# Gated recurrence and top-1 experts on one core: held blank writes, eleven x rows, an early tile of expert 0, and the general path's loop behind the experts

## The chip, the cores and the metric

The kernel runs on one core of a Trainium2 chip. The metric is the device time of one execution in microseconds, from the first to the last instruction of the program with what starts and ends it. Before the change three runs took 733.5, 734.44 and 731.06 us (median 733.5). A further run was profiled: it took 731.12 us, and its span in the profile, first to last instruction, is 729.4 us. All positions in time below are microseconds of that span.

## The reference

Two blocks follow each other.

```
# gateloop: B, H, S, D = 4, 8, 768, 48
mag = sqrt(a_re^2 + a_im^2); a *= min(mag, 0.999) / (mag + 1e-6)
for t in range(S):                       # a complex state D x D per (b, h)
    S_re, S_im = a_re*S_re - a_im*S_im + k[t] v[t]^T, a_re*S_im + a_im*S_re
    y[t] = q[t] . S_re
# x = y as (B*S, H*D) = (3072, 384)
# switch, top 1 of E = 8 experts, F = 1024
logits = x @ w_gate; e = argmax(logits); gate = softmax(logits)[e]
out = gate * (relu(x @ w1[e]) @ w2[e])
```

All data are fp32. Each of the 3,072 tokens goes through exactly one expert.

## The kernel before

**Attention stage.** The recurrence is computed in chunks of 128 steps (C = 6 chunks per sequence). For one batch b at a time, `front` (L369) scans the gates on VectorE: fifteen steps of multiplies, 576 and 288 wide, and one add each; `fix` (L413) carries the result over blocks, once for each of the three tiles t of 128 rows of heads x dimension, `fold` (L432) multiplies q and k with the scanned gates and writes the products `pk`, from which DMAs on SyncE load the tiles `KX` and `QX`, and `attention` (L491) does the scores, masks and outputs on TensorE for each group of heads. `load_gates` (L336) brings the gates a_re and a_im of a batch in four pairs of DMAs, and `limit` (L343) normalises them on ScalarE and VectorE.

Each chunk's outputs are gathered into an `xf` row buffer: 128 tokens by 384 values plus the gate and the token number. There are `ROWS = C + 2 = 8` of these buffers (L36), taken in turn: chunk number b*C + c uses buffer (b*C + c) % ROWS, so that a buffer is written again eight chunks later, and then only when its move has read it.

**Router.** `send` (L616) takes the logits of a batch, finds expert, gate and a place (slot) for each token in the DRAM table `sorted_x`, and moves each chunk's 128 rows there by an indirect DMA on POOL (`away`, L661 to L671). Batches 0 to 2 are sent whole, batch 3 in three pieces of three, two and one chunks (L201). `free_row` holds how many rows of each expert are taken so far. Each expert has room for CAP = 448 rows. Rows that no token fills must be blank, and so, once before the first move, eight DMAs on POOL write blank rows over the eight experts' places (L681, 675.5 KB each, from the tile `empty`). In the list of steps each blank write is put after a step of batch 1's front, but that order is only a due time for the planner: in the program the writes wait only for the memset of `empty`.

**Order.** None of this is issued as it is written: every step is an `Op` with an engine, a modelled duration, what it needs and which buffers it reuses. `in_time` (L85) simulates the engines, and the steps are emitted in the order of the simulated starts (L704). `InOrder` (L127) keeps that order on each engine. Its one line, L135, is therefore the line of nearly all planned instructions in the profile; tiles tell them apart. Within an engine's queue an instruction that waits holds back all behind it.

**Junction.** Behind the last send, `fine` says whether the fast path's assumptions held, and one matmul (`bank<-ones_f,fine`) sums it to `trips`, 0 or 1. The weights of experts 0 to 2 are fetched ahead (L700). Then `load` (L712) brings expert 0's 448 rows: three tiles of 128 on SyncE, the half tile in two DMAs on ScalarE's queue. `values_load` (L746) reads `trips` into a register of each engine. `with tc.For_i(0, n_gen, 1)` (L1007) repeats the whole computation in a general way when `trips` is 1; with the inputs here it runs no time.

**Expert stage** (L1015 to L1054). For each expert: `turned` (L723) transposes the 448 rows on TensorE (twelve transposes), 24 products with w1 give h in eight tiles of 448 columns (`h_ps`), which ScalarE (even) and VectorE (odd) evict with relu to `ht`; three o tiles of 384 columns and one half tile (`o_ps`) follow, each scaled by the gate on eviction and moved to `out` by an indirect DMA on POOL (`to_out`, L736; the token numbers are in `to`). The next expert's rows are loaded and turned inside the loop, and `fetch(e + 3)` brings weights. An fp32 matmul is two records in the trace. PSUM comes from pools: 2 buffers for transposes, 4 for h, 2 for o.

Of the kernel before, what the change touches and what calls it, by code (L numbers as in the profile page):

```python
# [19 lines left out]
C = S // 128  # L20
# [15 lines left out]
ROWS = C + 2  # L36
CAP = 448
LEAST = 1e-20
# [100 lines left out]
def gateloop_then_moe(ctx, tc, q, k, a_re, a_im, v, wg, w1, w2, out):  # L139
# [106 lines left out]

    with ExitStack() as att:
        one = att.enter_context(tc.tile_pool(name="one", bufs=1))
        bank = att.enter_context(tc.tile_pool(name="bank", bufs=1, space=PSUM))
# [18 lines left out]
        QXs = [buf(f"QX{i}", C, 256) for i in range(RING)]  # L268
        KTs = [buf(f"kt{i}", 3, 128) for i in range(2)]
        for i in range(RING):  # L270
            nc.gpsimd.memset(KXs[i][R2:128, :], 0.0)
            nc.gpsimd.memset(QXs[i][R2:128, :, :], 0.0)
            nc.gpsimd.memset(QXs[i][0:R2, :, 128 + R2:], 0.0)
# [22 lines left out]
        ps = [bank.tile([128, 512], FP32, name=f"bank{i}") for i in range(8)]  # L296
# [194 lines left out]
        def attention(b, g):  # L491
# [24 lines left out]
            for c in range(C):  # L516
# [51 lines left out]
                if c < C - 1:  # L568
                    ws, st_readers = ring("st", 2)

                    def turned(c=c, wk=wk, st=st):
                        for i in range(n):
                            vals = vb[c].rearrange("p h e -> p (h e)")[:, first[i]:first[i] + 128]
                            if c > 0:
                                T.matmul(sp_ps[:, i, :], lhsT=QX[i][:, c, 128:], rhs=sts[st[0]][:, i, :], start=True, stop=False)
                            T.matmul(sp_ps[:, i, :], lhsT=KTs[wk][:, i, :], rhs=vals, start=(c == 0), stop=True)
# [35 lines left out]
        def send_all():  # L612
            while sent_later:
                send(*sent_later.pop(0))

        def send(k, b, c0, n, lg):  # L616
# [40 lines left out]
            state["free row"], state["count"] = f, [f]  # L657
            state["lg"] = [d]
            moves = []
            for i in range(n):  # L660
# [8 lines left out]
                move = pool_dma(8.0, away, [s, m, *state["blank"]] + state["row", b, c0 + i])  # L669
                moves += [move, m]  # L670
                state["xf", (b * C + c0 + i) % ROWS] = [move, state["x row", b, c0 + i]]  # L671
            state["sent", k % 2], state["sent"] = [s, gate, f, *moves], [s, gate, f]
# [3 lines left out]
        for b in range(B):  # L676
            steps = front(b, range(G))
            fixed = [fix(t) for t in range(G)]
            if b == 1:

                state["blank"] = [pool_dma(8.0, lambda e=e: nc.gpsimd.dma_start(  # L681
                    sorted_x[e * N:e * N + CAP].rearrange("(u p) w -> p u w", p=64), bc(empty[:, None, :], [64, CAP // 64, WS])), [o])
                    for e, o in enumerate((steps + sum(fixed, []))[3::2][:E])]
                send_all()
# [14 lines left out]
        dve(1, lambda: V.tensor_scalar(out=trips, in0=ps[7][0:1, 511:512], scalar1=127.5, scalar2=None, op0=ALU.is_lt), [o])  # L699
        for e in range(3):  # L700
# [7 lines left out]
    with ExitStack() as ms:  # L708
# [4 lines left out]
        def load(e, xs, half_queue=nc.sync):  # L713
            r = e * N
            nc.sync.dma_start(xs[:, 0:TT, :], sorted_x[r:r + TT * 128].rearrange("(t p) w -> p t w", p=128))
# [4 lines left out]
        def room():  # L720
            return xp.tile([128, TT + 1, WS], FP32, name="xs")

        def turned(xs):  # L723
            xt = mp.tile([128, DT, CAP], FP32, name="xt")
            for d in range(DT):
                ps = psX.tile([128, CAP], FP32, name="xt_ps")
                for i in range(TT + 1):
                    n = min(128, CAP - i * 128)
                    T.transpose(ps[:, i * 128:i * 128 + n], xs[0:n, i, d * 128:d * 128 + 128], ident[0:n, 0:n])
                if d == 1:  # L730
                    nc.scalar.copy(xt[:, d, :], ps)
                else:
                    nc.vector.tensor_copy(xt[:, d, :], ps)
            return xt
# [10 lines left out]
        xs = load(0, room(), nc.scalar)  # L745
        n_gen = nc.values_load(trips[0:1, 0:1], min_val=0, max_val=1, skip_runtime_bounds_check_because="0 or 1")  # L746


        def general():
            gs = ExitStack()  # L750
            gen = gs.enter_context(tc.tile_pool(name="gen", bufs=1))
            with ExitStack() as fs:
                fp = fs.enter_context(tc.tile_pool(name="fp", bufs=1))
                fps = fs.enter_context(tc.tile_pool(name="fps", bufs=1, space=PSUM))
                lg_all = gen.tile([128, NT, E], FP32, name="lg_all")
                zrow = fp.tile([1, W], FP32, name="zrow")
                nc.vector.memset(zrow, 0.0)
                nc.sync.dma_start(x_hbm[N:N + 1, :], zrow)
                BG = B * G
                state = fp.tile([128, 2, BG, D], FP32, name="state")  # L760
                nc.gpsimd.memset(state, 0.0)

                own_i = fp.tile([128, G, H], I32, name="own_i")
                nc.gpsimd.iota(own_i, pattern=[[128, G], [-D, H]], base=0, channel_multiplier=1)
                own_f = fp.tile([128, G, H], FP32, name="own_f")
                nc.vector.tensor_copy(own_f, own_i)
                own = fp.tile([128, G, H], FP32, name="own")
                nc.vector.tensor_scalar(out=own, in0=own_f, scalar1=0.0, scalar2=None, op0=ALU.is_ge)
                nc.vector.tensor_scalar(out=own_f, in0=own_f, scalar1=float(D), scalar2=None, op0=ALU.is_lt)
                tt(own, own, own_f, ALU.mult)  # L770
                x_tok = x_hbm[0:N, 0:DM].rearrange("(b s) (h e) -> s h b e", b=B, e=D)
                with tc.For_i(0, S // BL, 1) as i0:
                    a = fp.tile([128, 2, BG, BL], FP32, name="fa")
                    qk = fp.tile([128, 2, BG, BL], FP32, name="fqk")
                    for b in range(B):
                        for t in range(G):
                            for o, src in ((a[:, 0], a_re), (a[:, 1], a_im)):
                                nc.sync.dma_start(o[:, b * G + t, :], src[b].rearrange("p j (t m) -> t m p j", t=G)[t, ds(i0, 1)])
                            for u, src in enumerate((q, k)):
                                nc.sync.dma_start(qk[:, u, b * G + t, :], src[b, :, t].rearrange("p j m -> m p j")[ds(i0, 1)])  # L780
                    vt = fp.tile([128, BG, BL, D], FP32, name="vt")
                    for b in range(B):
                        for t in range(G):
                            for h, p0, n, d0 in segments(t):
                                src = v[b].rearrange("(m j) (h w) -> m h j w", j=BL, w=D)[ds(i0, 1), h]
                                nc.sync.dma_start(vt[p0:p0 + n, b * G + t], src.to_broadcast([n, BL, D]))
                    af = a.rearrange("p u n t -> p u (n t)")
                    sq = fp.tile([128, 2, BG * BL], FP32, name="fsq")
                    mag = fp.tile([128, BG * BL], FP32, name="fmag")
                    den = fp.tile([128, BG * BL], FP32, name="fden")  # L790
                    nc.scalar.activation(sq, af, func=ACT.Square)
                    tt(mag, sq[:, 0, :], sq[:, 1, :], ALU.add)
                    nc.scalar.activation(mag, mag, func=ACT.Sqrt)
                    nc.vector.tensor_scalar_add(den, mag, 1e-6)
                    nc.vector.reciprocal(den, den)
                    stt(den, mag, 0.999, den, ALU.min, ALU.mult)
                    tt(af, af, bc(den[:, None, :], list(af.shape)), ALU.mult)
                    for t in range(BL):
                        shape = [128, BG, D]

                        def col(x, u):
                            return bc(x[:, u, :, t:t + 1], shape)
                        z = {}
                        for x in range(2):
                            for y in range(2):
                                z[x, y] = fp.tile(shape, FP32, name=f"fz{x}{y}")
                                tt(z[x, y], state[:, x], col(a, y), ALU.mult)
                        vv = fp.tile(shape, FP32, name="fvv")
                        tt(vv, vt[:, :, t, :], col(qk, 1), ALU.mult)
                        tt(state[:, 0], z[0, 0], z[1, 1], ALU.subtract)  # L810
                        tt(state[:, 1], z[0, 1], z[1, 0], ALU.add)
                        tt(state[:, 0], state[:, 0], vv, ALU.add)
                        tt(vv, state[:, 0], col(qk, 0), ALU.mult)
                        yt = fps.tile([H, B, D], FP32, name="yt")
                        for g in range(G):
# [281 lines left out]
```

## Time and profile before

| engine | busy us | share of the span | instructions |
|---|---|---|---|
| TensorE (PE) | 570.0 | 78% | 3050 |
| TensorE weight load (PEld) | 423.8 | 58% | 3050 |
| VectorE (DVE) | 366.3 | 50% | 726 |
| ScalarE (ACT) | 297.9 | 41% | 926 |
| GpSimd (POOL) | 92.5 | 13% | 101 |

DMA moved 89.79 MB at a mean of 123 GB/s. The mean granted clock of TensorE was 0.955. The stages, by the trace: the first matmul starts at 100.90, the last one of the attention stage at 398.18, the expert stage's first transposes at 408.47, the last out DMA is issued at 721.81. From one expert's last out DMA to the next one's, in steady state, are 38.75 us.

How to read it: the page cuts the span into 40 slices and gives busy tenths of each engine. A group row gives a line, an engine, an operation and its tiles (out<-in), then busy us and mean ns. A timeline row gives start, duration, engine, line, operation and tiles, and in brackets the idle time of that engine ahead of it and what released it ("<-DMA x" is a transfer, "<-ACT x" an instruction of ScalarE). A row of a window gives the stretch, its length, then the busy time (and number) of PE, PEld, DVE, ACT and POOL, TensorE's granted clock, the busy share of the 16 DMA engines and GB/s. SPq and POOLq are the queues from which SyncE and POOL issue DMAs.

### The profile page before, as it was taken

How to read it: one execution, taken by the hardware profiler on the slowest of the kernel's cores; microseconds unless marked ns; L12 is line 12 of the kernel's file. 1: busy time of each engine (PE TensorE's matmuls, PEld its weight loads, DVE VectorE, ACT ScalarE, POOL GpSimd, SP SyncE). 2: the span in 40 equal slices, each digit the busy share in tenths (PEclk: the TensorE clock that was granted, in tenths of full speed). 3: DMA queues.
4: the chain of work that ended last, by engine and by line, in shares of the span. 5: the costliest groups of instructions: out<-in, count | busy, mean ns of one | idle time of the engine just before them, and what ended most of it. 6: DMA issues, size and time to landing. Idle time of an engine off the chain costs nothing. (4 is left out here: it accounts for less than half of the span.)

```text
span 729.4 us, 8993 instructions
## 1 busy us (share of the span) xinstructions
PE 570.0 (78%) x3050; PEld 423.8 (58%) x3050; DVE 366.3 (50%) x726; ACT 297.9 (41%) x926; POOL 92.5 (13%) x101
## 2 busy tenths in 40 slices
PE   0000049985479989988996599999999999999995
PEld 0000039985469978987896355565655555555553
DVE  3929999999979999997413110201011111111010
ACT  4525369976869689568653110101010101001000
POOL 9300000000340023003003002010101111010101
PEclk9999999995879999998999699999999999999999
DMA  6982078327661578369921322323232324020000
GB/s 192 222 193 65 21 198 208 107 67 187 161 190 51 131 197 268 113 148 225 310 123 67 91 86 76 131 82 129 102 141 109 141 100 148 12 68 12 18 12 24
DMA packets 59718, 89.79 MB, mean 123 GB/s; under 512 B 5885, under 2 KB 48015, under 8 KB 57616
## 3 DMA queue, kind: packets, MB, share of 16 engines
q1 hardware_dynamic: 54640, 73.94, 34.6%
q0 software_dynamic: 4864, 15.00, 7.1%
q8 instruction: 26, 0.43, 0.2%
q10 hardware_dynamic: 160, 0.20, 0.1%
q14 instruction: 28, 0.23, 0.1%
HBM read 55.10 MB, written 15.78 MB: 97 GB/s over the span
## 5 line engine op out<-in xcount | busy, mean ns | idle before, releaser
L135 PE MATMUL bank<-QX,KX 128*128 128x224 f32 (+1 forms) x384 | 89.2, 369 | 113.1 <-DMA KX<-pk 100.9
L135 PE MATMUL h_ps<-xt,big 128*128 128x448 f32 x384 | 148.1, 546 | 0.0
L135 PE MATMUL o_ps<-big,ht 128*128 128x384 f32 (+1 forms) x640 | 147.9, 424 | 0.0
L135 PEld LDWEIGHTS bank<-QX,KX 128*128 128x128 f32 x384 | 70.4, 208 | 116.8 <-issue 100.9
L135 PEld LDWEIGHTS o_ps<-big,ht 128*128 128x128 f32 (+1 forms) x640 | 90.1, 169 | 56.1 <-issue 4.7
L135 PEld LDWEIGHTS h_ps<-xt,big 128*128 128x128 f32 x384 | 73.0, 192 | 71.3 <-issue 71.2
L135 PE MATMUL bank<-st,QX 128*128 128x128 f32 x576 | 110.2, 279 | 2.2 <-ACT st L135 2.2
L135 ACT ACTIVATE big<-big 128x576 f32<-128x576 f32 (+2 forms) x92 | 79.2, 871 | 43.0 <-DVE big L135 23.2
L135 PEld LDWEIGHTS bank<-st,QX 128*128 128x128 f32 x576 | 88.4, 195 | 3.1 <-ACT st L135 3.1
L135 PE MATMUL bank<-vb,am 128*128 128x128 f32 x384 | 74.0, 284 | 14.0 <-ACT xf L135 13.9
L135 ACT ACTIVATE QX<-diag,KX 96x48 f32<-96x48 f32 x320 | 80.4, 328 | 7.3 <-DMA KX<-pk 7.1
L662 POOL DMA_INDIRECT sorted_x<-xf,slot x24 | 38.8, 1616 | 336.8 <-DVE big L135 170.0
L1030 ACT ACTIVATE ht<-h_ps 128x448 f32<-128x448 f32 x32 | 17.4, 544 | 131.9 <-PE h_ps L135 131.9
L1028 DVE TENSOR_SCALAR ht<-h_ps 128x448 f32<-128x448 f32 x32 | 20.0, 624 | 99.2 <-PE h_ps L135 99.0
L135 PEld LDWEIGHTS bank<-vb,am 128*128 128x128 f32 x384 | 59.7, 196 | 16.6 <-ACT xf L135 16.1
L135 DVE TENSOR_TENSOR big<-big,big 128x576 f32<-128x576 f32 (+1 forms) x72 | 62.9, 884 | 0.5
L135 DVE TENSOR_TENSOR big<-big 128x288 f32<-128x288 f32 (+2 forms) x104 | 60.9, 600 | 1.1 <-ACT big L135 0.6
L135 PE MATMUL bank<-vb,kt 128*128 128x128 f32 x320 | 59.3, 277 | 1.7 <-ACT kt L135 1.7
L1041 ACT ACTIVATE yo<-o_ps,xs 128x384 f32<-128x384 f32 x16 | 9.3, 581 | 124.8 <-PE o_ps L135 124.8
L135 DVE TENSOR_TENSOR am<-bank,causal 128x256 f32<-128x256 f32 (+1 forms) x120 | 42.7, 362 | 34.0 <-PE bank L135 33.9
L737 POOL DMA_INDIRECT out_dram<-yo,to x24 | 23.4, 974 | 279.3 <-ACT yo L1041 245.8
L135 PEld LDWEIGHTS bank<-vb,kt 128*128 128x128 f32 x320 | 47.6, 192 | 2.3 <-ACT kt L135 1.9
(105 smaller groups left out, 500.5 us busy)
## 6 DMA issues: line engine op xcount, KB each, us to landing
big<-in_moe_w_dram SPq DMA_DIRECT2D x16, 1536.0 KB, 6.6
KX<-pk SPq DMA_DIRECT2D x48, 146.2 KB, 4.4
QX<-pk SPq DMA_DIRECT2D x48, 144.0 KB, 3.8
sorted_x<-empty POOLq DMA_DIRECT2D x8, 675.5 KB, 11.7
xs<-sorted_x SPq DMA_DIRECT2D x8, 579.0 KB, 8.4
big<-in_a_re_dram SPq DMA_DIRECT2D x16, 288.0 KB, 3.4
big<-in_a_im_dram SPq DMA_DIRECT2D x16, 288.0 KB
qt<-in_q_dram SPq DMA_DIRECT2D x12, 384.0 KB, 4.7
```

The lines of the kernel that those rows point to most:

```text
L135: return lambda *a, **kw: self.tc.keep_in_program_order(f(*a, **kw))
L662: move = nc.gpsimd.indirect_dma_start(out=sorted_x[:, :], out_offset=bass.IndirectOffsetOnAxis(ap=slot[:, i:i + 1], axis=0), in_=xfs[(b * ...
L737: move = nc.gpsimd.indirect_dma_start(out=rows, out_offset=bass.IndirectOffsetOnAxis(ap=index, axis=0), in_=y, in_offset=None, bounds_chec ...
L1028: nc.vector.tensor_scalar_max(ht[:, f, :], h, 0.0)
L1030: nc.scalar.activation(ht[:, f, :], h, func=ACT.Relu)
L1041: nc.scalar.activation(y, o, func=ACT.Copy, scale=xs[:, i, DM:DM + 1])
```

## The change

There are four edits.

1. *Blank writes.* Each of the eight DMAs gets a semaphore dependency on the VectorE instruction that was emitted last before it. The steps that they are put behind change too: the adds 2, 5, 8, 11 and 14 of batch 1's front and the last step of each of its three fixes.
2. *Buffers.* Eleven xf rows in place of eight; a row of `QX` becomes 224 wide in place of 256, and the memset of its pad (six on POOL) goes. The matmul that read the pad as weights reads 32 columns of the next chunk in its place, into outputs that are not used. The modelled time of a move goes from 8 to 10.
3. *Early tile.* After batch 2's send, `free_row` of expert 0 is raised to at least 128 (one more VectorE instruction), so that batch 3 writes no row below 128. `load_early` reads these 128 rows on SyncE, the last item of the attention stage in that queue, into the free tail of a weight buffer; `turn_early` turns them (three transposes, one ScalarE copy), ahead of the last send's ranks on TensorE. Behind the `fine` matmul follow the tile's h (24 products of 128 columns), four evictions each on ScalarE and VectorE, its o (eight of 384), the scaling on VectorE and an out DMA. Expert 0 then has 320 rows left: nine transposes, h of 320 columns, two tiles and the half one.
4. *Loop.* The loop of the general path and the function stand behind the experts, and `values_load` stands in the pass of expert 6. PSUM pools become eight banks that both stages share, with the same counts. The rewrite of blank rows inside the general path goes.

On VectorE's queue the order behind `trips` is now: `to_e`, early evictions f1 and f3, the `to` of expert 0, f5 and f7, the `to` of expert 1, then y_e and the copies of `xt`. On SyncE the loads of experts 0 and 1 follow each other directly.

```diff
-ROWS = C + 2
+ROWS = C + 5
+EARLY = 128
...
-        QXs = [buf(f"QX{i}", C, 256) for i in range(RING)]
+        QXs = [buf(f"QX{i}", C, 128 + R2) for i in range(RING)]
...
-            nc.gpsimd.memset(QXs[i][0:R2, :, 128 + R2:], 0.0)
...
+        def load_early():
+            l = dma(5.0, lambda: Q.dma_start(xs_e, sorted_x[0:EARLY]), state["moves"], state["z", 0] + state["z", 1])
+            state["early"] = l
+        def turn_early():
+            def across_early():
+                for d in range(DT):
+                    T.transpose(px_ps[:, d, :], xs_e[:, d * 128:d * 128 + 128], ident)
+            px = pe(6, across_early, [state["early"]], state.get("px", []), first=B * G)
+            c = act(DM, lambda: A.copy(xt_e, px_ps), [px], first=6)
...
+            if b == B - 2:
+                f = dve(1, lambda: V.tensor_scalar_max(free_row[:, k + 1, 0:1], free_row[:, k + 1, 0:1], float(EARLY)), [f])
...
-                move = pool_dma(8.0, away, [s, m, *state["blank"]] + state["row", b, c0 + i])
+                move = pool_dma(10.0, away, [s, m, *state["blank"]] + state["row", b, c0 + i])
...
-                    for e, o in enumerate((steps + sum(fixed, []))[3::2][:E])]
+                def blank(e):
+                    step = next(i for i in reversed(nc.cur_bb.bb.instructions) if i.engine == nc.vector.engine)
+                    tc.add_manual_dep(nc.gpsimd.dma_start(sorted_x[e * N:e * N + CAP].rearrange("(u p) w -> p u w", p=64),
+                                                          bc(empty[:, None, :], [64, CAP // 64, WS])).ins, step.name,
+                                      mybir.DependencyInfo(mybir.DependencyClass.Sync, mybir.DependencyReason.DATA), reason="not before")
+                state["blank"] = [pool_dma(8.0, lambda e=e: blank(e), [o]) for e, o in enumerate((steps[1::3] + sum(fixed, [])[1::2])[:E])]
...
+        def first_tile(e):
+            return EARLY // 128 if e == 0 else 0
+        def bank_of(kind):
+            own = {"x": (6, 7), "h": (2, 3, 4, 5), "o": (0, 1)}[kind]
...
+        to_e = mp.tile([128, 1], I32, name="to_e", bufs=1)
+        nc.vector.tensor_copy(to_e, xs_e[:, DM + 1:WS])
+        for i in range(2):
+            h = bank_of("h").rearrange("p (f w) -> p f w", w=128)
+            for f in range(4):
+                for d in range(DT):
+                    T.matmul(h[:, f, :], lhsT=w1t[:, d, (4 * i + f) * 128:(4 * i + f) * 128 + 128], rhs=xt_e[:, d, :],
+                             start=(d == 0), stop=(d == DT - 1))
+            for f in range(4):
+                if f % 2:
+                    nc.vector.tensor_scalar_max(ht_e[4 * i + f], h[:, f, :], 0.0)
+                else:
+                    nc.scalar.activation(ht_e[4 * i + f], h[:, f, :], func=ACT.Relu)
+        o = bank_of("o")[:, 0:DM]
+        for f in range(FT):
+            T.matmul(o, lhsT=ht_e[f], rhs=w2t[:, f, :], start=(f == 0), stop=(f == FT - 1))
+        nc.vector.tensor_scalar_mul(y_e, o, xs_e[:, DM:DM + 1])
+        to_out(y_e, out, to_e)
...
-        with tc.For_i(0, n_gen, 1):
-            general()
-            load(0, xs)
...
+            if e == E - 2:
+                n_gen = nc.values_load(trips[0:1, 0:1], min_val=0, max_val=1, skip_runtime_bounds_check_because="0 or 1")
...
+    with tc.For_i(0, n_gen, 1):
+        general()
```

## The prediction

> **What bounds the kernel now.** First the busy tenths in 40 slices (18.2 us each):
>
> ```profile
> PE   0000049985479989988996599999999999999995
> DVE  3929999999979999997413110201011111111010
> PEclk9999999995879999998999699999999999999999
> DMA  6982078327661578369921322323232324020000
> ```
>
> Three stages with different limits. Up to slice 17 VectorE is full but for one hole in slice 2, while TensorE starts late (100.9 us) and has holes; slices 18 to 20 are TensorE's; from slice 22 the experts keep TensorE full. So a gain counts if it shortens VectorE's chain before about 330 us, or TensorE's time after it. I then read the timelines at the holes.
>
> The hole of slice 2 (VectorE's and ScalarE's timelines, SyncE's issues, the issue table, one window with the DMA share next to last):
>
> ```profile
> 28.73 0.38 SPq L135 DMA_DIRECT2D big<-in_a_re_dram  x1
> 29.15 2.35 SPq L135 DMA_DIRECT2D big<-in_a_im_dram  x1
> 50.44 1.74 ACT L135 ACTIVATE big<-big 128x1152 f32<-128x1152 f32 x2 [14.89 <-DMA big<-in_a_im_dram]
> 51.63 0.76 DVE L135 SCALAR_TENSOR_TENSOR big<-big 128x576 f32<-128x576 f32 x1 [12.82 <-ACT big L135]
> sorted_x<-empty POOLq DMA_DIRECT2D x8, 675.5 KB, 11.7
> 26.00:28.00 2.00, 0.00 (x0) 0.00 (x0) 2.00 (x5) 0.73 (x3) 0.00 (x0) 1.00 1.00 198
> ```
>
> Gate loads issued at 29 us land at 50; behind them VectorE waits 12.82 us. Meanwhile the eight blank writes, issued from 18.25 us, fill the DMA engines (share 1.00).
>
> The xf rows and the junction to the experts (VectorE, POOL, TensorE):
>
> ```profile
> 206.57 0.76 DVE L135 SCALAR_TENSOR_TENSOR big<-big 128x576 f32<-128x576 f32 x1 [3.51 <-ACT big L135]
> 193.80 8.50 POOL L662 DMA_INDIRECT sorted_x<-xf,slot  x1 [169.72 <-DVE big L135]
> 398.18 0.19 PE L135 MATMUL bank<-ones_f,fine 128*1 128x1 f32 x2 [0.93 <-DVE fine L135]
> 408.47 3.45 PE L135 MATMUL xt_ps<-ident,xs 128*128 128x128 f32 x12 [10.11 <-SPq L1007]
> 411.86 19.92 PE L135 MATMUL h_ps<-xt,big 128*128 128x448 f32 x48
> 398.00:399.00 1.00, 0.19 (x2) 0.09 (x2) 0.27 (x2) 0.00 (x0) 0.69 (x2) 0.54 0.23 87
> 414.00:415.00 1.00, 1.00 (x2) 0.34 (x1) 0.00 (x0) 0.00 (x0) 0.00 (x0) 0.50 1.12 401
> 416.00:417.00 1.00, 1.00 (x4) 0.44 (x4) 0.00 (x0) 0.55 (x1) 0.00 (x0) 1.00 0.05 6
> ```
>
> TensorE stands still for 10.11 us: last moves, xs load, loop. The windows (column before the DMA share: TensorE's clock) show half clock until 415.
>
> **What the Trainium skill says.** "TensorE: Matmul & The Clock Gate", What's actually happening: TensorE runs at half clock after an idle window and returns to full after some 3.4 us of continuous work. The trace agrees: 0.54 at 398, 0.50 at 414, 1.00 by 416, about 3.2 us after the first h matmul. "DMA: Bandwidth & Descriptors", Issuing engines are not separate DMA queues: transfers of all issuers share the same engines. It agrees: SyncE's gate loads took 21 us beside POOL's blanks. "Runtime: NRT & Kernel Launch", Instruction fetch mechanics: a jump outside the fetched instructions waits for a fetch. The trace can't separate that from the loop's other costs.
>
> **Part 1, blanks held** (semaphores on VectorE's adds 2, 5, 8, 11, 14 of batch 1's front and on the three fixes). Queue 0 holds 43.8% of the 16 engines in 0 to 60 us: 26.3 us of full DMA, 3.3 per blank. Bytes issued on hardware queues before 28.7 us are about 4.3 MB; at the 314 to 367 GB/s of these stretches they drain by some 22 us. The load of 28.7 then lands after some 3.4 us, as a_re does in the issue table, and the next (issued 38.84) by 43, before ScalarE needs it at 44.5. The whole hole goes: **−12.8**, and the chain behind it is solid until 203 us.
>
> The same 26.3 us come back at 117 to 173 (old clock). There the DMA share has mean 0.49 over 116 to 176, so they fit as a whole; in 116 to 140 alone five blanks (16.5 us) meet 10.3 us of free time, so KX, QX and gate loads run late by up to 6 us. TensorE has such slack (it waits for VectorE 6 us at 169 to 175), VectorE has less. From 0 to +6; I take **+1.5**, since the stretch 144 to 160 is nearly empty (shares 0.07 to 0.23) and lets the queue drain. Queued behind the waiting blanks on POOL are only batch 0's moves, due at 193.8 − 12.8 = 181; the last blank is released near 173 − 12.8 = 160 and landed in 11.7 us: 172. Hidden. The six pad memsets that go (0.26 us each) lay on POOL, which has no work then: nothing.
>
> **Part 2, eleven xf rows, narrower QX.** ScalarE waits 4.18 us for row 0's move (at 205.6), and VectorE 3.51 us behind it. With eleven rows reuse comes at batch 1's chunk 5, not 2; but on ScalarE's queue the copy that waits stands at nearly the same place (row 289, was 286), with one activation of the gates now ahead of it. Below, a gain of all 3.51 us (a little more if TensorE's hole of 12.55 counts); above 0. I take **−2**.
>
> **Part 3, early tile.** Added on TensorE behind the `fine` matmul: 24 h products of 128 columns (48 records at 0.1115 us, the full-clock pitch of that width) = 5.35, and 8 o products of 384 (16 at 0.321) = 5.15: 10.5 us. Removed from expert 0: three transposes, an h pass of 128 of 448 columns (18.0 → 12.9 us) and one o tile (5.15). The early work lies in the hole that was idle: its data are in before the last moves. At half clock for its first 3 to 3.4 us it needs some 3 us more: from 398.4 to 411.9. Then nine transposes (1.7), h 12.9, turning expert 1 (1.3), two tiles 10.3, half tile 2.6, about 0.6 of gaps: 441.3, against 452.7 now (its last out DMA): **−11.4**. Ends: −14.1 if the clock stays high; −6 if VectorE's queue holds it. On ScalarE the half loads (issued at 401.8, after the last moves) stand ahead of ht_e f0. On VectorE `to_e` waits for the same moves, the `to` of experts 0 and 1 stand ahead of ht_e f5, f7 and y_e and wait for the xs loads (402 to 407 or later). Early h takes until 405 or so, which covers most of these waits.
>
> The added early transposes (three), ScalarE copy, VectorE maximum and out DMA lie before the last send or behind TensorE: about nothing. The early load on SyncE is last in its queue behind the fetches; its 128 rows land during batch 3, which is TensorE's 64 us. The maximum can shift expert 0's slots by empty rows only.
>
> **Part 4, loop behind the experts.** VectorE's loop steps took 0.8 us (407.43 to 408.20), plus a jump; SyncE waited 3.8 us in it. At the end nothing covers it: 0.5 to 4, I take **+1.4**. The load of `trips` (684 ns on TensorE at 398.6) now stands between experts 6 and 7: 0 to 0.7, **+0.5**. Banks keep their counts (2, 4, 2): nothing. Its removal at 407 is in part 3.
>
> **Sum:** −12.8 + 1.5 − 2 − 11.4 + 1.4 + 0.5 = −22.8 against the profiled span 729.4: 706.6. That run took 731.1 (1.7 more than its span): 708.3. From the median 733.5: 710.7. Forecast **709.5**.
>
> **Rivals.**
> - *Junction only half filled* (VectorE's `to` ahead of the early evictions, SyncE's two loads side by side: about 1.2 MB): −6 instead of −11.4: 715. For: the order of VectorE's queue; against: the loads were short in the trace (DMA busy 403 to 406).
> - *More than the sum*: clock high (−14.1), all 3.5 at 203, no collision: 709.5 − 2.7 − 1.5 − 1.5 = 704; with TensorE's small holes near 251 to 279, 701.
> - *Collision*: KX, QX and gate loads late beside the blanks by more than the slack, at most all 16 us of overrun and later stalls; at +10 to +12: 719. For: share 1.05 at 120 to 124; against: 0.49 in the mean.
> - *The hold doesn't do what it says*: the blanks still start early enough to meet the gate loads, or other loads fill the DMA alone: no −12.8, no +1.5: 721.
> - *Slower than before*: the blanks become the new wait. All moves of batch 0 wait for all eight, and POOL issues in order; if the eighth lands after 181, each us more holds the first move (8.5 us itself), then ScalarE's xf copy, then VectorE and TensorE. To end above 733.5 needs 24 us of such delay, a landing near 205, which is 45 us from release; before, the slowest landed in 26 us under full load. Then about 738.
>
> **How the numbers follow.** Forecast 0.42, half-filled junction 0.18, more 0.14, collision 0.12, no hold 0.08, slower 0.04; 0.02 for the unforeseen. The range from 700 to 722 leaves out the slower case and tails, about 0.15. About 0.5% (3.7 us) is what a measurement can tell from no change. Faster 0.93, same 0.03, slower 0.04.
>
> **What would show it.** Part 1: no idle time of VectorE before 51 us, gate loads landing in about 3.4 us, blanks from some 105 us on. Wrong if a hole appears in VectorE between 105 and 170 or the first move is later than 182. Part 2: no xf copy waiting for a move. Part 3: h matmuls of 128 columns right behind `fine`, expert 0's last out DMA about 11 us closer to `fine` than the present 54; wrong if o_ps waits for VectorE or ScalarE between them. Part 4: the time from the last out DMA to the end, now 6.6 us (722.8 to 729.4), grows by 1 to 2. Wrong altogether if some expert's step of 38.75 us changes, or batch 3's 64 us grow.

## The result, and the profile after

Four runs of the changed kernel took 724.67 us in the median (721.07 to 725.23), four of the kernel before on the same chip 732.9: a ratio of 0.9878, with a 95% interval from 0.9838 to 0.9919. The change is faster by some 8 us; the forecast was 709.5, and 724.67 lies above the range that ended at 722. Its profiled execution took 725.23 us with a span of 723.3, against 729.4 before: 6.1 less in the two traces that are compared here. (The trace of before is of a run 1.8 us under its median; the sums below are those of the two traces.)

The busy tenths of the page, after the change:

```profile
PE   0000099875799659997998899999999999999991
DVE  3999999898999999995423111111010101011100
PEclk9999999986999879999999999999999999999996
DMA  5321579469841775478921324242423312010000
```

VectorE's hole in slice 2 is gone and TensorE starts most of a slice earlier. But TensorE shows new dents in slices 8, 13 and 14, and in the last slice it stands still, at a falling clock. Five marks in the traces cut the difference into pieces. "am, batch 1" is the first product with `am` of batch 1, the moment when TensorE has that batch's scores, masks and state together.

| mark | before | after | difference | change of it |
|---|---|---|---|---|
| first matmul | 100.90 | 89.38 | −11.5 | −11.5 |
| am, batch 1 | 180.62 | 176.59 | −4.0 | +7.5 |
| `fine` matmul | 398.18 | 394.13 | −4.05 | 0.0 |
| expert 0's last out DMA | 452.95 | 439.52 | −13.4 | −9.4 |
| expert 7's last out DMA | 721.81 | 708.75 | −13.1 | +0.4 |
| end | 729.40 | 723.26 | −6.1 | +6.9 |

So two pieces came about as forecast (start and junction), and two costs were far larger: 7.5 us between the first matmul and batch 1, and 6.9 at the end.

**Between the first matmul and batch 1.** The timelines of POOL, ScalarE, VectorE and TensorE of the changed kernel (start, duration, engine, line, operation; in brackets the idle time ahead and its releaser):

```profile
106.99 0.92 POOL L710 DMA_DIRECT2D sorted_x<-empty  x1 [91.94 <-DVE am L136]
112.16 0.74 POOL L710 DMA_DIRECT2D sorted_x<-empty  x1 [4.25 <-DVE am L136]
...
167.69 0.70 POOL L710 DMA_DIRECT2D sorted_x<-empty  x1 [10.93 <-DVE fl L136]
127.28 1.16 ACT L136 ACTIVATE big<-big 128x1152 f32<-128x1152 f32 x1 [3.62 <-DMA big<-in_a_im_dram]
128.47 0.76 DVE L136 SCALAR_TENSOR_TENSOR big<-big 128x576 f32<-128x576 f32 x1 [2.51 <-ACT big L136]
170.51 3.80 ACT L136 ACTIVATE QX<-diag,KX 96x48 f32<-96x48 f32 x16 [2.46 <-DMA KX<-pk]
171.21 5.55 PE L136 MATMUL bank<-QX,KX 128*128 128x224 f32 x16 [11.19 <-ACT QX L136]
```

and TensorE's row for the same scores in the kernel before:

```profile
175.43 5.35 PE L135 MATMUL bank<-QX,KX 128*128 128x224 f32 x16 [6.11 <-ACT QX L135]
```

The hold works as written: the first blank goes at 107, the last at 168. What was a wait for a gate load at 51 us is now a wait for gate loads at 127 and for KX at 170, and TensorE stands idle for 11.19 us ahead of batch 1's scores (6.11 before). Not all of this idle time is the late KX: a run below, without a blank in this stretch, still has 9.35 us of it.

**The junction**, TensorE's and VectorE's timelines, and the window of 400 to 410 (TensorE's clock stands just before the DMA share):

```profile
395.69 5.73 PE L136 MATMUL bank<-big,big 128*128 128x128 f32 x42
401.25 3.39 PE L136 MATMUL bank<-big 128*128 128x384 f32 x10
406.37 0.91 PE L136 MATMUL bank<-big 128*128 128x384 f32 x2 [1.73 <-DVE big L799]
408.41 1.92 PE L136 MATMUL bank<-ident,xs 128*128 128x128 f32 x9
405.88 0.16 DVE L155 SCALAR_TENSOR_TENSOR to<-xs,upper 128x1 int32<-128x1 f32 x1 [4.20 <-DMA xs<-sorted_x]
406.03 0.28 DVE L799 TENSOR_SCALAR big<-bank 128x128 f32<-128x128 f32 x1
400.00:410.00 10.00, 8.16 (x37) 4.99 (x35) 2.46 (x10) 1.50 (x5) 0.49 (x1) 1.00 0.50 138
```

The early tile fills the hole. Its first products run from 394.25 at half clock, but in this window the clock is full. VectorE's `to` of expert 0 stood ahead of an early eviction and waited 4.20 us for xs, and the o tile waited behind it.

**The end**, POOL's timeline and then the view of the loop's line (durations in ns: least, median, most; then the first and last start in us) and of the program's last line:

```profile
708.75 0.97 POOL L777 DMA_INDIRECT out_dram<-yh,to  x1 [1.58 <-DVE yh L845]
...
L1108 POOLq EVENT_SEMAPHORE  x17: 17/43/43, 709.2 to 716.9; - x17
L1108 POOLq COMPARE_BRANCH  x3: 38/41/49, 709.2 to 717.0; - x3
L1108 POOLq INC_SWDGE_SEM  x1: 1467/1467/1467, 711.8 to 711.8; - x1
...
L1147 POOLq DRAIN  x3: 40/103/5302, 717.1 to 723.0; - x3
```

POOL enters the loop at 709.2, waits for the last out DMA to land (711.7), steps its DMA semaphores for 1.47 us, jumps, goes through twelve semaphores and leaves at 717.0. The other engines wait in the loop too, so it acts as a barrier. Only then does its last drain begin, which takes 5.3 us. Before the change the drain began right behind the last out DMA:

```profile
L1093 POOLq DRAIN  x3: 40/247/6516, 721.6 to 729.1; - x3
```

### The profile page after: what moved, and what is told of

Same layout as the page of the kernel before. It is cut to its first block, busy times and chain, and to the rows that moved or that the text cites. A ratio compares the mean times of both kernels' runs of the same rounds, so it can differ in the third digit from the quotient of the medians.

```text
span 723.3 us, 9083 instructions
## 1 busy us (share of the span) xinstructions
PE 568.9 (79%) x3098; PEld 427.5 (59%) x3098; DVE 369.4 (51%) x733; ACT 296.2 (41%) x929; POOL 85.2 (12%) x95
## 5 line engine op out<-in xcount | busy, mean ns | idle before, releaser
L136 PE MATMUL bank<-big,ht 128*128 128x384 f32 (+1 forms) x624 | 142.7, 423 | 0.0
L136 PE MATMUL bank<-xt,big 128*128 128x448 f32 (+1 forms) x384 | 141.3, 528 | 0.0
L136 PEld LDWEIGHTS bank<-big,ht 128*128 128x128 f32 (+1 forms) x624 | 87.0, 168 | 53.9 <-issue 4.7
L136 PEld LDWEIGHTS bank<-xt,big 128*128 128x128 f32 x384 | 72.3, 190 | 65.5 <-issue 61.8
L824 DVE TENSOR_SCALAR ht<-bank 128x448 f32<-128x448 f32 (+1 forms) x32 | 19.4, 607 | 97.6 <-PE bank L136 97.4
L826 ACT ACTIVATE ht<-bank 128x448 f32<-128x448 f32 (+1 forms) x32 | 17.0, 530 | 125.9 <-PE bank L136 125.9
L136 DVE TENSOR_TENSOR big<-big,big 128x576 f32<-128x576 f32 (+1 forms) x72 | 62.9, 884 | 0.4
L136 PE MATMUL bank<-vb,kt 128*128 128x128 f32 x320 | 61.4, 286 | 0.9 <-ACT kt L136 0.9
L136 DVE TENSOR_TENSOR am<-bank,causal 128x256 f32<-128x256 f32 x120 | 42.7, 363 | 34.9 <-PE bank L136 26.7
L837 ACT ACTIVATE yo<-bank,xs 128x384 f32<-128x384 f32 x15 | 8.7, 580 | 120.6 <-PE bank L136 120.6
L686 POOL DMA_INDIRECT sorted_x<-xf,slot x24 | 34.1, 1422 | 193.0 <-DVE big L136 77.8
```

What stands on the lines that cost most here:

```text
L136: return lambda *a, **kw: self.tc.keep_in_program_order(f(*a, **kw))
L686: move = nc.gpsimd.indirect_dma_start(out=sorted_x[:, :], out_offset=bass.IndirectOffsetOnAxis(ap=slot[:, i:i + 1], axis=0), in_=xfs[(b * ...
L824: nc.vector.tensor_scalar_max(ht[:, f, cols], h, 0.0)
L826: nc.scalar.activation(ht[:, f, cols], h, func=ACT.Relu)
L837: nc.scalar.activation(y, o, func=ACT.Copy, scale=xs[:, i, DM:DM + 1])
```

## The experiments

Each run is compared with the changed kernel (724.67) and with the kernel before, whose median over the runs shared with each group lay between 732.4 and 733.4. In four traces with the same attention stage, `fine` lies between 392.9 and 395.0, and the changed kernel itself was timed in four runs alone; a difference of a few us is therefore read from the marks of the traces as well as from the times.

### The loop

```diff
-    with tc.For_i(0, n_gen, 1):
-        general()
```

> The changed kernel without the general path's loop at its end (the loop runs no time with these inputs; the read of trips stays). Theory: the loop stands bare behind the last out DMA and costs its landing wait, POOL's semaphore step and jump, some 7 us, before POOL's final drain can begin: 717.7, last out DMA to end back near 6.6 us. Rival: the final drain waits for the out DMAs anyway and hides the loop; the extra 7 us come from somewhere else: 724 to 725.

Measured: 717.35 us (716.07 to 720.02), ratio to before 0.9782 (0.9742 to 0.9823). The run leaves out the general path, so it prices the loop and is no kernel to use. Its trace shows no read of `trips` either, though the read stands in the program; in the change this read lies on POOL from 708.5 to 709.0, ahead of a wait that ends at 711.7, so it costs nothing there. From the last out DMA (709.26) to the end of the span (716.4) it takes 7.1 us in place of 14.5. POOL's last drain, in the view of the program's last line, is again as long as before the change:

```profile
709.26 0.97 POOL L777 DMA_INDIRECT out_dram<-yh,to  x1 [1.57 <-DVE yh L845]
...
L1145 POOLq DRAIN  x3: 40/113/6517, 709.0 to 716.1; - x3
```

The cost is more than the loop's own steps: the drain covers the landing of the last DMA when nothing is between them (6.5 us from the issue), and still takes 5.3 us when it begins long after that landing. The loop takes away this overlap. The theory stands.

The loop put between the attention stage and the early tile, which then reads its rows again if the loop has run, with VectorE in the written order, as in a run of the last section of experiments:

```diff
+        n_gen = nc.values_load(trips[0:1, 0:1], ...)
+        banks.close()
+        with tc.For_i(0, n_gen, 1):
+            general()
+            nc.sync.dma_start(xs_e, sorted_x[0:EARLY])
...
         xs = load(0, nc.scalar)
```

> The changed kernel with VectorE's order as in the run before, and the loop between the attention stage and the early tile (the early rows are read again in it). Theory: the bare end costs 7 us and goes; at the junction the loop waits for the last moves and costs about 4 to 5 before the early tile: 719 to 721, TensorE idle some 8 us behind fine. Rival: the half clock and the late early tile cost as much as the end: 722 to 725.

Measured: 724.73 us (0.9899, 0.9871 to 0.9928). The end is short (7.1 us), but the early tile starts 6.47 us late, by TensorE's timeline, and from `fine` to expert 0's last out DMA it takes 50.9 us, 7.7 more than in the same order without it. Besides the wait, some 1.1 us go to a half clock that lasts longer (the 48 records take 8.17 us, there 7.05):

```profile
395.04 0.19 PE L136 MATMUL bank<-ones_f,fine 128*1 128x1 f32 x2 [0.93 <-DVE fine L136]
...
401.70 8.17 PE L136 MATMUL bank<-big,big 128*128 128x128 f32 x48 [6.47 <-issue]
```

The rival is right here: bare at the junction, the loop costs what it costs at the end. In the kernel before it was cheap because TensorE waited there for xs anyway: without the loop and without the early tile it still waits 8.15 us there (a run of the last section), with the loop 10.11.

### The blank writes

Hold alone, in the kernel before (the same steps and semaphores as in the change):

> The kernel before with the hold of the blank writes alone (same steps as in the changed kernel). Theory: the start gains 11 us and the collision at 107 to 170 us takes about 8 back: 729 to 731. The prediction's own sum for this part: -11.3, 721 to 722. Rival: all is given back or more: 733 or above.

Measured: 723.96 us (0.9865, 0.9832 to 0.9897), so 9.4 less than before in the median; my figure was too small. In the trace it is −12.5 at the first matmul, −5.9 at batch 1's am, −5.8 at `fine` and −5.7 at the end. The start gains all that was forecast, and half of it goes back before batch 1. The trace of this run is 1.5 above its median and that of before 2.3 under its group's median, which accounts for the rest. The 6.6 us that go back appear here with eight rows and the old order of steps, so they don't come from the other edits. And the hold alone is as fast as the whole change (724.67): what the early tile gains, the bare loop costs again.

The same blanks in batch 0, in the changed kernel:

```diff
-            if b == 1:
+            if b == 0:
...
-                    ... enumerate((steps[1::3] + sum(fixed, [])[1::2])[:E])]
-                send_all()
+                    ... enumerate(steps[9:15] + sum(fixed, [])[0:2])]
+            if b == 1:
+                send_all()
```

> The changed kernel with the eight held blank writes released in batch 0's front and first fix (44 to 70 us, where the DMA share is under 0.4), in place of batch 1's. Theory: in the changed kernel the blanks at 107 to 168 us make KX, QX and gate loads late and give back about 8 us of the 11 gained at the start; moved, no such holes: 717 to 719, first move near 183 in place of 190.9. Rival: the loss between 110 and 190 us comes from the other order of steps (eleven rows, move time 10), not from the blanks: 724 to 725.

Measured: 723.91 us (0.9865, 0.9831 to 0.9899), no better than the change. The holes at 118 to 135 are gone, but the mistake of the kernel before was made again in another place. ScalarE's timeline:

```profile
72.46 2.54 ACT L136 ACTIVATE big<-big 128x1152 f32<-128x1152 f32 x2 [9.27 <-DMA big<-in_a_im_dram]
```

The first matmul comes at 93.25, 3.9 later than in the change, batch 1's am at 174.1, 2.5 earlier, `fine` 1.3 earlier. Its time is nearly the rival's, but the holes went and another came, so it spoke for neither theory. The bytes themselves were changed next (with these inputs alone, where tokens fill all rows below 256):

```diff
-  sorted_x[e * N:e * N + CAP] ... bc(empty[:, None, :], [64, CAP // 64, WS])
+  sorted_x[e * N + 256:e * N + CAP] ... bc(empty[:, None, :], [64, 3, WS])
```

> The changed kernel with blank writes of rows 256 to 447 of each expert alone (3 of 7 of the bytes; rows 0 to 255 are all filled by tokens with these inputs), so 11 us of full DMA in place of 26. Theory: the blanks' bytes are what batch 1's start loses (first product with am of batch 1 at -4.0 us against the kernel before, after -11.5 at the first matmul); with 3/7 of them it stands at -7 to -9, and, if that passes on to the end, 720 to 722. Rival: TensorE is the bound from batch 2 on and its order there swallows it: batch 1 earlier, end the same, 724 to 725.

Measured: 719.73 us (0.9824, 0.9797 to 0.985), 4.9 less than the change for 15 us less of DMA (4/7 of the prediction's 26.3). Batch 1's am comes at 170.4, 10.2 ahead of before, and `fine` at 389.7, 4.4 ahead of the change. So the blanks' bytes are what batch 1's start loses, and most of the gain passes on to the end; the rival, that TensorE's order swallows it, falls.

All eight full blanks behind the last gate load of batch 1:

```diff
+            if b == 0:
...
+                    ... enumerate(steps[14:15] * 6 + sum(fixed, [])[0:2])]
```

> The changed kernel with all eight full blank writes released behind the last steps of batch 0's front and its first fix (56 to 68 us), into the stretch 60 to 78 us in which the DMA engines are idle, after the last gate load of batch 1. 26 us of DMA then run to about 85 and meet only the first KX and QX loads. Theory: those are late by up to 7 us at the first matmul (95 or so), nothing is lost afterwards: batch 1's first product with am 6 to 8 us before that of the kernel before; 721 to 723. Rival: DMA volume costs the same wherever it lies: 724 to 725.

Measured: 731.73 us (0.9988, 0.997 to 1.0005): as slow as before. Both expectations missed. I had looked for a stretch in which the DMA engines were idle, 60 to 78, and not for who issues next. Eight blanks keep the share at 0.97 from 56 to beyond 90 us, and the loads of q and k, then of KX, stand in them; VectorE's timeline and the issue table of that stretch (KB each, median us to landing):

```profile
95.26 0.96 DVE L136 TENSOR_TENSOR pk<-big,qt 128x768 f32<-128x768 f32 x1 [9.17 <-DMA qt<-in_q_dram]
98.41 0.96 DVE L136 TENSOR_TENSOR fl<-fl,kt_in 128x768 f32<-128x768 f32 x1 [1.43 <-DMA kt_in<-in_k_dram]
103.83 0.96 DVE L136 SCALAR_TENSOR_TENSOR fs<-big 128x768 f32<-128x768 f32 x1 [3.60 <-ACT big L136]
...
qt<-in_q_dram SPq DMA_DIRECT2D x2, 384.0 KB, 14.2
```

In the same place, blanks of rows 320 to 447 alone, which do fit, with two VectorE steps that send the kernel to its general path if an expert has fewer than 320 rows:

```diff
-  sorted_x[e * N:e * N + CAP] ... [64, CAP // 64, WS]
+  sorted_x[e * N + FULL:e * N + CAP] ... [64, (CAP - FULL) // 64, WS]     # FULL = 320
...
+        o = dve(E, lambda: V.tensor_reduce(fine[:, 1:2], fit, axis=AX, op=ALU.min), [o])
+        o = dve(1, lambda: vstt(fine[:, 2:3], fine[:, 1:2], float(FULL), fine[:, 2:3], ALU.is_ge, ALU.mult), [o])
```

> The run before with blank writes of rows 320 to 447 alone, and two more VectorE steps by which trips also becomes 1 when an expert has fewer than 320 rows (the fewest here is 338). 7.5 us of DMA fit into 60 to 78 us. Theory: the start's 12 us pass through whole: first matmul at 88.5, batch 1's am at -11, fine near 387; 716 to 718. Rival: batch 1 takes back its usual 5 us even with no blanks in it: 720 to 722.

Measured: 720.37 us (0.9835, 0.9808 to 0.9861). The first matmul (89.43) and batch 1's am (169.62, −11.0) are where the theory has them: with no blank beside it, the stretch between them gives back 0.5 us in place of 7.5. What this stretch looks like with and without blanks is shown by one row of the windows, 106 to 176 us (busy time of TensorE, its weight load, VectorE, ScalarE and POOL; then clock, DMA share, GB/s), first of the changed kernel:

```profile
106.00:176.00 70.00, 54.07 (x389) 51.97 (x388) 64.16 (x121) 51.59 (x167) 5.90 (x8) 0.85 0.74 195
```

and then of this run:

```profile
106.00:176.00 70.00, 58.02 (x439) 56.26 (x438) 69.51 (x131) 56.52 (x188) 0.00 (x0) 0.90 0.53 138
```

The mean DMA share of 0.74 is far from full, and still VectorE loses 5.4 us of its 70. TensorE's wait ahead of batch 1's scores shrinks only from 11.19 to 9.35 us:

```profile
164.61 5.17 PE L137 MATMUL bank<-QX,KX 128*128 128x224 f32 x16 [9.35 <-ACT QX L137]
```

so the late KX accounts for some 2 of the 7.5 us. The rest lies ahead of it, with VectorE's 2.51 us at 128 as the largest hole. The time lies in the rival's range, but not for the rival's reason, since batch 1 took back only 0.5. The end came 2 us later than forecast: `fine` is at 389.05, not 387, since some 2 us of the gain are lost after batch 1's am, as in the run with rows 256 to 447. Why is open.

### The xf rows

> The changed kernel with eight xf rows in place of eleven. Theory: the hole behind the first moves comes back (VectorE 3.5 us, TensorE up to 12 us near 200 us) and the end moves by 3 to 5: 728 to 730. Rival: the copy that waits stands at the same place of ScalarE's queue, so rows are worth nothing: 724 to 725.5.

Measured: 726.61 us with runs from 721.78 to 728.05 (0.9883, 0.9836 to 0.9931): between the two figures, and not decided. The part alone, in the kernel before (ROWS = C + 5, QX 224 wide, move time 10):

> The kernel before with part 2 alone (eleven xf rows, QX 224 wide, move time 10 in the plan). Theory: TensorE's hole of 12.55 us in batch 1 goes, but what it gains there is lost at the start of batch 2, where TensorE waits for VectorE's masks, so that the time from batch 1's first product with am to fine stays at 217 to 221 us and the end within 1.5 of before. The prediction: -2 (0 to -3.5).

Measured: 731.4 us in 22 runs, 0.9982 (0.9969 to 0.9995): 1.3 us less, with an interval from 0.4 to 2.3, not more. In its trace `fine` stands at 398.24, before at 398.18. TensorE's timelines show the exchange, first the hole of the kernel before, then this run, with one row of its ScalarE:

```profile
205.93 0.80 PE L135 MATMUL bank<-vb,am 128*128 128x128 f32 x2 [12.55 <-ACT xf L135]
...
206.12 0.49 PE L135 MATMUL bank<-vb,am 128*128 128x128 f32 x2 [0.28 <-ACT xf L135]
...
253.97 6.49 PE L135 MATMUL bank<-QX,KX 128*128 128x224 f32 x16 [4.82 <-DMA KX<-pk]
266.24 1.22 PE L135 MATMUL bank<-vb,am 128*128 128x128 f32 x4 [5.77 <-DVE am L135]
...
359.62 1.01 ACT L135 ACTIVATE QX<-diag,KX 96x48 f32<-96x48 f32 x4 [8.14 <-DMA KX<-pk]
362.80 0.80 PE L135 MATMUL bank<-vb,am 128*128 128x128 f32 x2 [7.15 <-ACT xf L135]
```

The hole of 12.55 us at 205.93 is gone and batch 1's logits end 8 us earlier (249.2, before 257.2), but TensorE then waits 4.82 us for batch 2's KX and 5.77 for VectorE's masks, and batch 2's first product with am comes at 266.2, before at 263.0. From there the run is ahead again: 62.5 us to batch 3's first product with am, before 72.2. Batch 3 takes that back: 69.5 us to `fine`, before 63.0, because ScalarE waits 8.14 us for KX at 359 and TensorE behind it. The change shows the same pattern (62.6, then 68.1), and so does the run without the early tile (63.3, then 70.8), while the hold alone keeps the old one (72.1, then 62.9). So it is edit 2 that lengthens batch 3, not the early tile. Which part of edit 2 is open: the run with eight rows, which keeps the narrow QX and the move time of 10, has 72.1 us there too, so it is not the number of rows alone. In all these traces it takes 217 to 221 us from batch 1's am to `fine`, whatever the rows.

### The early tile and VectorE's order

Without the early tile (loop at the end, all else as in the change):

> The changed kernel without the early tile (no load, turn, maximum, products; expert 0 with all 448 rows), loop at the end. Theory: from fine to expert 0's last out DMA it takes 52 to 53 us (45.4 in the changed kernel, 54.8 before), and the attention stage ends as in the changed kernel: 731 to 732. Rival: the early tile's items in the plan are what makes batch 3 slower (68.1 us from its first product with am, 63.0 before), and attention ends 4 us earlier: 727 to 728.

Measured: 733.99 us in 20 runs (1.002, 1.0006 to 1.0035), 9.3 more than the change. From `fine` to expert 0's last out DMA it takes 53.8 us (45.4 with the tile, 54.8 before), and the attention stage is not faster, so the rival falls. TensorE waits for xs, loop or no loop:

```profile
404.20 3.43 PE L136 MATMUL bank<-ident,xs 128*128 128x128 f32 x12 [8.15 <-DMA xs<-sorted_x]
```

So the tile is worth 8 to 9 us, the loop's removal from the junction about 1, and the change without the tile is no faster than before.

VectorE held to the written order in the expert stage (`DV = InOrder(tc, nc.vector)` in the place of `nc.vector` there):

> The changed kernel with VectorE held to the written order in the expert stage, so that the reads of xs (to) of experts 0 and 1 stand behind the early evictions. Theory: the early o tile no longer waits for the load of xs, TensorE goes into the transposes when xs has landed, near 406 in place of 408.4: -2, 722 to 723. Rival: the transposes wait as long for xs: 724 to 725.

Measured: 723.81 us (0.9887, 0.9864 to 0.991); against the change's 0.9878 this decides nothing by time. In the trace the transposes follow `fine` after 12.2 us in place of 14.3, and expert 0's last out DMA after 43.3 in place of 45.4, the 2 us of the theory; the o tile (the first row) is no longer interrupted:

```profile
399.86 4.04 PE L136 MATMUL bank<-big 128*128 128x384 f32 x12
403.74 1.45 PE L136 MATMUL bank<-big,big 128*128 128x384 f32 x4
405.02 1.91 PE L136 MATMUL bank<-ident,xs 128*128 128x128 f32 x9
```

The order costs this only where xs lands late: in the run with eight rows, which has the change's order, xs came 8.0 us behind `fine` in place of 11.75, the o tile did not wait, and it also took 43.3 us to expert 0's last out DMA.

Both improvements together, the blanks of rows 320 to 447 and VectorE's order:

> The run before with VectorE in the written order in the expert stage: a further -2 at the junction: 714 to 716. Rival: the order gains nothing: as the run before.

Measured: 719.08 us (717.5 to 720.08), ratio 0.981 (0.9785 to 0.9835). It is faster than both kernels, by some 13.7 us than before and 5.6 than the change, though 3 above the upper figure expected, since its base was. Beside that base (720.37) the order's part is 1.3 us, too little to decide by time; in the traces expert 0's last out DMA comes 1.2 us nearer to `fine`. The loop is still bare at its end.

## Why the prediction was wrong, step by step

Two terms of its sum failed, each beyond its own bound: what the blanks cost in their new place, and what the loop costs at the end. The rest was off by 2 us or less a term.

- *Start, −12.8.* Held: −11.5 at the first matmul (−12.5 with the hold alone). Gate loads no longer wait for blanks.
- *The same DMA work at 117 to 173, "+1.5", from 0 to +6.* This term failed first: it measured +7.5. The forecast reasoned with a mean DMA share of 0.49 and an empty stretch at 144 to 160 in which the queue would drain. But a gate load that is late at 127 stopped ScalarE for 3.62 us and then VectorE for 2.51, which has no slack, and the last three blanks fell on 148 to 168 and made batch 1's KX late, for which ScalarE and behind it TensorE waited. The runs with fewer bytes show that it is the blanks: 15 us less of their DMA gave 5 us back, and blanks that meet no load gave back nearly all. The rival *collision* (719, at +10 to +12) was the nearest for this part.
- *The rows, −2.* Too large, though within its range: 0.0 from batch 1's am to `fine` in the change, and −1.3 (0.4 to 2.3) for the part alone. The hole that was removed lay in TensorE's way, but the masks for batch 2 come from VectorE's queue no earlier, so TensorE waits there instead, and in the part's own run once more in batch 3, behind a late KX. The forecast priced a hole and not the next wait behind it.
- *Early tile, −11.4.* The mechanism held, with −9.4. The half clock cost less than the 3 us taken: the 48 records of 128 columns took 7.17 us, not 5.35, so 1.8. The forecast's own 3 to 3.4 us at half speed lose only half of that time, 1.5 to 1.7; "some 3" was a slip. But the time to full clock is less sure than it reads there: in the trace of before TensorE works without a gap from 408.47, on transposes first, and the clock is still 0.50 until 415, so it took over 6.5 us of work and not 3.2; in the run with the loop ahead of the tile the records took 8.17 us. The wait of the o tile behind `to`, which the rival *half filled* had named, cost 2.1 us.
- *Loop at the end, +1.4, from 0.5 to 4.* This is the second term that failed: +6.9 in the marks, 7.3 by the run without it. The forecast took VectorE's loop steps (0.8 us) and a jump for the price and did not follow POOL, which has the DMA's landing, the semaphore step (1.47) and its jump to go through, and its drain still to come. SyncE's 3.8 us in the loop, seen and set aside, was a sign.
- *The load of `trips`, +0.5.* Inside its range, at 0: TensorE reads it at 669.8, and the two steps around this, 38.73 and 36.47 us from one expert's last out DMA to the next one's, are as before. The +0.4 of the table lies in the step from expert 1 to 2, and five other runs with the same read in the same place don't have it.
- *Signs named ahead.* Four of those that were to show it wrong came: VectorE's hole between 105 and 170, a first move later than 182 (190.94, released by VectorE, since batch 1 was late, not by the blanks), an o tile that waits for VectorE, and a longer batch 3. The last was to mean "wrong altogether"; the run with edit 2 alone has it too, so it comes from that edit, and the sum over the three batches stayed (217.5 us in both traces).

The shortfall of the sum is 16.7 us (−22.8 against −6.1): 6.0 by the blanks, 5.5 by the end, 2.0 each by rows and junction, 1.3 by the start. The first two are 11.5 together and bring the forecast of 709.5 to 721, just inside the range; with the 4 us of rows and junction the time falls outside. The slower case (blanks landing after 181) did not come: the last blank was issued at 168, and in the median a blank landed 6.6 us after its issue.

Open stay: why some runs lose 2 us after batch 1's am and others don't; and why the stage from there takes 217 to 221 us with eight rows and with eleven, though its waits lie in other batches.

## What to carry to other kernels

Moving a transfer away from one wait is only half of the step: list the loads that its new place meets, and who stands still for each, since a mean DMA share of 0.74 already cost 7 us here; fewer bytes beat both other places that were tried. A loop that runs no time was not free here: POOL waited in it for its outstanding DMA, so price it on the engine that issued the DMAs, and look for a place where the engines wait anyway. And the gain of a hole ends at the next thing that the freed engine waits for, so look one wait further before adding it.

## What the hardware showed that was not expected

- A loop of no iterations costs 7.3 us behind the last out DMA and 7.7 between the attention stage and the early tile; POOL, the last engine to leave it, is in it from 709.2 to 717.0. The Trainium skill, "Runtime: NRT & Kernel Launch", Instruction fetch mechanics, names a fetch at a jump out of the fetched instructions; POOL's steps show 2.6 us between its branch at 713.27 and its next semaphore at 715.91. In the trace, six transfers of the instruction queues fall between 709 and 717, one of them inside this gap, and none at the end of the run without the loop. That fits a fetch; for which engine each was, the trace doesn't say.
- POOL's last drain takes 6.5 us when it stands right behind the last out DMA, and 5.3 us when that DMA landed 5.4 us earlier.
- The DMA engines carry eight blank writes (5.5 MB) at some 190 GB/s with a share of 0.97: they take over 30 us together with the loads that meet them, and a load of 384 KB in them needs 14.2 us, against a median of 4.3 in the run with the small blanks there.
